# A hand-written order of steps exchanged: contiguous PSUM reads, fewer folded rows, two summed units, five output folds on GpSimd

## The chip, the cores and the metric

One NeuronCore of a Trainium2 chip runs the kernel. The metric is the device time in microseconds (us). Beside it stands the span, from the first to the last instruction of one profiled execution. The engines are TensorE (PE in the profile; PEld is its weight load), VectorE (DVE), ScalarE (ACT), GpSimd (POOL) and SyncE (SP, which here only issues DMAs).

## The reference

`x` has 2048 rows and 1024 columns in bf16. Two spectral filters are applied to it and mixed by a gate for each row:

```
g = sigmoid((x * gate_w).sum(-1, keepdims=True))
a = irfft2(rfft2(x) * (A_w_r + 1j * A_w_i))     # A_ref(x, A_w_r, A_w_i)
b = irfft2(rfft2(x) * (B_w_r + 1j * B_w_i))     # B_ref(x, B_w_r, B_w_i)
return g * a + (1 - g) * b
```

## The kernel before, in words

All transforms are products with constant matrices. Columns are folded so that even and odd frequencies (`par` 0 and 1) are handled apart, and the frequencies along the rows are split into 8 units for each parity, 16 units `n` in all (0 to 7 even, 8 to 15 odd).

The work is a list of tokens, `ORDER`, written out by hand. `run` (L587) takes them one by one and emits each step's instructions; each engine then runs its own in that order, waiting only for its data and its buffers. So the list fixes the order within each engine and each DMA queue, not the times. A token is a letter, its indices and, behind the colon, the engines of its copies out of PSUM or of its sum (A ScalarE, V VectorE, Q GpSimd). The steps are these:

- `V` (L277): a row block of `x` is folded by VectorE, a sum and a difference of its halves (L280, L281). `r` and `f` (L284, the same code under two letters): first transform of one row block, both parities; 16 matmuls of 128 columns if folded (L297), 16 of 256 if not (L306). `E`/`O`: the same for two row blocks, even and odd parity apart, 32 matmuls of 128 columns each (L309). Results are cast to `y`, two casts a token.
- `y`, `h`, `g`: gate weights (nine small VectorE operations, L322 to L333), the gate's own transform (32 matmuls and a small DMA by GpSimd, L341 to L347), the sigmoid and its table `EAB` (L350 to L361).
- `F` (L365): second forward transform of a unit into `T`, two casts; for even units GpSimd first negates a column of the weights (L369). `d` (L417): the edge columns of even units, small matmuls and two small VectorE operations (L430), which must follow GpSimd's negation. `G` (L382): third forward transform into `X`, two casts.
- `c` (L407): the complex product with both filters' weights, one VectorE operation over 4096 elements of each partition, into a buffer `p`. `a` (L434): sums two of a unit's four products on VectorE (L439), after which `i.0` and `i.1` each leave out one of four terms of matmuls (L448), 8 matmuls in all.
- `i` (L442): first inverse transform, part 0 or 1 of a unit, two casts into `rl`; after part 1 a DMA writes the unit to DRAM (`sc`, L461).
- `q` (L467): fetches a quarter of four units back from DRAM in another layout, on SP's queue. `q1.1.x` needs units 12 to 15.
- `j` (L475): second inverse transform with the gate table, of parity and row group v (0 to 7), two casts into `V`. `k` (L489): third inverse transform, into a `p` buffer; then `s` (L541), the fold: a difference and a sum of 128x512 each (L551), after which the `p` buffer is free. `D` (L508): third and fold in one on PE, for odd parity, two casts (four half ones for v 7, of which one stays in PSUM). `t` (L553): sum and difference of the even and the odd part, then the output DMA.
- `w`: loads of weights whose buffers must first come free; `l`: a late constant (`IGU`, L252).

A `k` token comes in two forms. With `H` (L493) the two operands of the fold lie in two banks; one is cast to SBUF, through a view with a break in it (L501, L502), and the other is read by the fold straight from PSUM. Without `H` both are cast to SBUF, each from one whole bank, and the fold reads SBUF only:

```
apart = eng[0] == "H"
...
po = ps[r][:, s * 256:s * 256 + 256] if apart else ps[s][:, r * 256:r * 256 + 256]
...
if apart:
    evac(eng[1], cs[:, :, 0, :], pv[0])
    CSs[par, v] = cs[:, :, 0, :], pv[1]
else:
    evac2(eng, cs.rearrange("p s r d -> p s (r d)"), ps)
```

`BANKS` names the PSUM bank (of 8) for each use in turn, and `SLOTS` the buffer for each use of `T`, `X` (2 buffers each), `p`, `V` and `rl` (4 each); both are listed for one ORDER. In `p`, the first 16 uses are the products and the last 11 the `k` tokens. Weights and constants come on SP's queue in the order of L234 to L251.

Of the kernel before, what the change touches and what calls it, by code (L numbers as in the profile page):

```python
# [11 lines left out]
S = 2048  # L12
# [14 lines left out]


ORDER = """
V0 V1 V3 f0:AA f1:VA r2:AA V4 f3:VA V7 r5:AV V9 f4:AA r6:VA f7:VA r8:VA f9:VA r11:AA V13 r10:VA r12:AV f13:AA E14:VA y  # L30
O14:VA F0:AA F1:AA d0 G0:AA F2:AA d1 c0 G1:AA F3:AA d2 c1 G2:AA h F4:AA d3 G3:AA i0.0:AA i0.1:AA w7 c2 d4 c3 F5:AV
G4:AA i1.0:AA i2.0:VA c4 i2.1:AV d5 G5:AA i1.1:VA F6:AA F7:AA d6 w9 G6:AA i3.0:AA c5 i3.1:AV d7 F8:AA w8 c6 g0 i5.0:AA
G7:AV G8:AA w15 i5.1:AV q0.0.1 w14 c7 i6.0:AA q0.0.3 F9:AA F10:AA i4.0:AA c8 i6.1:VA i7.0:AA G9:AV G10:AV i4.1:VA
i7.1:AA c10 F11:AA q0.0.0 F12:AV c9 g1 G11:AA q0.0.2 c11 F13:AA G12:AA q0.1.0 i10.0:AA i9.0:AA i8.0:VA q0.1.3 i10.1:VV
i9.1:AA c12 i8.1:AA i11.0:VA G13:AA q0.1.1 q0.1.2 F14:VA F15:AA j0.0:AA c13 G14:AA i12.0:AV G15:AA i12.1:AA i11.1:AA
c14 c15 i13.0:AA i13.1:AA i14.0:AV a15.1:V i14.1:VV k0.0:HA j0.3:AA i15.0:AV i15.1:AV j0.2:AV j0.5:AA s0.0:V l q1.0.0
k0.3:HA j0.1:AA q1.1.0 s0.3:V j0.4:VA k0.5:HA j0.7:AA q1.0.1 s0.5:V k0.1:HA q1.1.1 k0.4:HA j0.6:AA s0.1:V k0.2:HA
s0.4:V q1.0.2 q1.1.2 k0.7:AA k0.6:HA j1.0:AA q1.1.3 s0.2:V j1.1:VA s0.6:V q1.0.3 k1.0:AA s0.7:V k1.1:HA s1.0:V j1.2:AA
j1.3:AA t0.2 s1.1:V D2:AA j1.4:AA k1.3:AA t2.2 t1.2 j1.5:AA s1.3:V D4:AA t3.2 t4.2 j1.6:AA D5:AA t5.2 D6:AA j1.7:AA
t6.0:S t6.1:S D7:AAAP t7.0:A t7.1:S  # L40
"""


# [1 line left out]


BANKS = """
01234567013245760321564371052634710562437162057143057623057146257146251427306517306514273065142763051427630154
62073154620731546207315426701354270615342706135427061354027364107236410752643071265401326470152647031564703125
64703125647  # L50
"""

SLOTS = {"T": "010101010101010101001010", "X": "0101010101001010", "p": "012302132103102130213021301",
         "V": "30123012302301230123", "rl": "0123012301231023102310321032103"}


def _bf16np(a):
# [99 lines left out]
def gated_mix(ctx, tc, x_in, we_in, wo_in, first_in, out):  # L157
    nc = tc.nc
    cn = make_constants()
    dr = {n: nc.inline_tensor(a, name=f"cst_{n.lower()}").ap() for n, a in cn.items() if n not in ("F1", "SG")}  # L160
# [13 lines left out]
    slots = {t: [wk.tile([P, w], BF16, name=f"{t}_{k}") for k in range(n)] for t, (n, w) in width.items()}  # L174
    order = {t: iter(v) for t, v in SLOTS.items()}

# [19 lines left out]
    F1 = const.tile([P, 208], BF16, name="f1")  # L196
# [10 lines left out]
    WF = const.tile([P, NT, 3, 64], BF16, name="wf")  # L207
    WI = const.tile([P, NT, 4, 64], BF16, name="wi")
# [5 lines left out]
    y = [Y[:, par] for par in range(2)]  # L214
# [3 lines left out]
    def load_w(n):  # L218
        par, u = n // NU, n % NU
        if n == 7:  # L220
            w = XP[0][:, 0:2064]
        elif 10 <= n < 14:
            w = wod[n - 10][:]
        else:
            k = {8: 0, 9: 1, 14: 2, 15: 3}.get(n, n)
            w = RP[k // 2][:, 2064 * (k % 2):2064 * (k % 2) + 2064]
        w = w[:, 0:8 * PIT[par]].rearrange("p (t a m) -> p t a m", t=2, a=4)
        nc.sync.dma_start(w, w_in[par][u])
        Ws[n] = w
# [4 lines left out]
    nc.sync.dma_start(fdv(0), dr["FD"][:, 0])  # L234
    nc.sync.dma_start(WF[:, 0:4], dr["WF"][:, 0:4])
    load_w(0)
    nc.sync.dma_start(WI[:, 0:4], dr["WI"][:, 0:4])
    load_w(1)
    load_w(2)
    nc.sync.dma_start(WF[:, 4:16], dr["WF"][:, 4:16])  # L240
    load_w(3)
    nc.sync.dma_start(WI[:, 4:16], dr["WI"][:, 4:16])
    load_w(4)
# [420 lines left out]
```

## Time and profile before

| | |
|---|---|
| time, median of 3 runs | 107.3 us (106.96 to 108.08) |
| profiled execution, its own time | 107.58 us |
| its span | 105.8 us |
| TensorE clock granted, mean | 0.996 |
| PE, ACT, DVE, POOL busy | 96.9, 93.6, 90.7, 10.1 us |
| DMA | 37.06 MB, mean 350 GB/s |

Busy time is a union: a PE that is marked busy can be waiting for a PSUM bank inside a matmul. In the timeline a row `start, length, engine, line, operation, out<-in, count` merges neighbours, and the square bracket gives the idle time ahead of it and what ended it. The mean of one instruction is longer than the step from one start to the next, because neighbours overlap.

### The profile page before, as it was taken

What the parts mean: (1) busy time and instruction counts of PE and PEld (TensorE: products, weight loads), DVE (VectorE), ACT (ScalarE), POOL (GpSimd) and SP (SyncE); (2) the same over time, 40 slices, a digit from 0 to 9 for tenths busy, and PEclk for the clock granted to TensorE, in tenths of its full rate; (3) what the DMA queues carried; (4) which work ended last, traced back from release to release, by engine and by line L of the source; (5) the groups of instructions that cost most, each with busy time, mean ns of one, the idle gap of its engine ahead of it and who ended that gap; (6) DMA issues with size and microseconds to landing.
All of it is one profiled execution on the core that took longest, in us unless ns stands there. A gap on an engine that the chain in (4) does not pass through costs nothing. (4 is left out here: it accounts for less than half of the span.)

```text
span 105.8 us, 3917 instructions
## 1 busy us (share of the span) xinstructions
PE 96.9 (92%) x1606; PEld 66.5 (63%) x1608; DVE 90.7 (86%) x141; ACT 93.6 (89%) x187; POOL 10.1 (10%) x14
## 2 busy tenths in 40 slices
PE   5999999969999999999999999999999698999740
PEld 2299998635655766655765567667898485754520
DVE  1399877388999989999999999999989969899870
ACT  5069999997999999999999999999999888999730
POOL 1000001179880000000000000000000000000000
PEclk9999999999999999999999999999999999999998
DMA  2999999999999999999999799969999899967993
GB/s 50 395 421 421 386 358 353 413 428 396 398 405 409 401 375 359 395 356 345 386 373 403 223 376 379 373 249 340 321 278 298 338 353 418 397 259 321 389 352 120
DMA packets 16737, 37.06 MB, mean 350 GB/s; under 512 B 1612, under 2 KB 10448, under 8 KB 15696
## 3 DMA queue, kind: packets, MB, share of 16 engines
q1 hardware_dynamic: 16128, 36.37, 92.3%
q10 hardware_dynamic: 560, 0.45, 1.3%
q8 instruction: 12, 0.20, 0.7%
q14 instruction: 5, 0.04, 0.1%
q0 software_dynamic: 32, 0.00, 0.0%
HBM read 24.23 MB, written 12.58 MB: 348 GB/s over the span
## 5 line engine op out<-in xcount | busy, mean ns | idle before, releaser
L453 PE MATMUL pt<-p,wi 64*64 64x512 bf16 x504 | 30.1, 377 | 0.2 <-DVE rl L265 0.2
L263 ACT CAST rl<-pt 128x512 bf16<-128x512 f32 x47 | 25.9, 732 | 0.1
L415 DVE TENSOR_TENSOR p<-X,ro 128x4096 bf16<-128x4096 bf16 x11 | 25.2, 2297 | 0.4 <-ACT X L263 0.3
L263 ACT CAST T<-pt 128x512 bf16<-128x512 f32 (+1 forms) x40 | 21.8, 636 | 0.9 <-PE pt L532 0.5
L453 PEld LDWEIGHTS <-wi 64*64 64x64 bf16 x504 | 15.3, 106 | 10.4 <-issue 0.9
L263 ACT CAST V<-pt 128x512 bf16<-128x512 f32 x29 | 17.3, 748 | 1.1 <-PE pt L483 1.1
L263 ACT CAST X<-pt 128x512 bf16<-128x512 f32 x29 | 16.8, 682 | 0.1
L375 PE MATMUL pt<-fd,y 128*128 128x256 bf16 x128 | 15.9, 273 | 0.0
L263 ACT CAST y<-pt 128x512 bf16<-128x512 f32 x21 | 10.9, 649 | 3.9 <-PE pt L297 3.4
L375 PEld LDWEIGHTS <-y 128*128 128x128 bf16 x128 | 11.6, 98 | 4.2 <-issue 2.9
L265 DVE CAST rl<-pt 128x512 bf16<-128x512 f32 x17 | 11.3, 683 | 0.0
L498 PE MATMUL pt<-ig,V 128*128 128x256 bf16 x88 | 10.8, 273 | 0.0
L369 POOL TENSOR_SCALAR ro<-ro 128x8 bf16<-128x8 bf16 x7 | 8.7, 1244 | 21.4 <-DMA ro<-in_we_dram 21.4
L574 DVE TENSOR_TENSOR rl<-wo,T 128x1024 bf16<-128x1024 bf16 (+1 forms) x16 | 8.9, 620 | 0.6 <-ACT T L263 0.6
L394 PE MATMUL pt<-T,wf 64*64 64x512 bf16 (+2 forms) x192 | 9.4, 307 | 0.0
L263 ACT CAST p<-pt 128x512 bf16<-128x512 f32 x14 | 9.4, 823 | 0.0
L551 DVE TENSOR_TENSOR wo<-p,pt 128x512 bf16<-128x512 bf16 x14 | 8.8, 682 | 0.6 <-ACT p L263 0.5
L415 DVE TENSOR_TENSOR p<-X,wo 128x4096 bf16<-128x4096 bf16 x4 | 9.1, 2285 | 0.0
L498 PEld LDWEIGHTS <-V 128*128 128x128 bf16 x88 | 8.0, 98 | 1.5 <-issue 0.4
L265 DVE CAST y<-pt 128x512 bf16<-128x512 f32 x11 | 7.2, 686 | 0.4 <-PE pt L309 0.4
L306 PE MATMUL pt<-f,xr 64*128 64x256 bf16 x112 | 7.0, 269 | 0.0
L394 PEld LDWEIGHTS <-wf 64*64 64x64 bf16 x192 | 4.7, 107 | 3.0 <-issue 0.4
(58 smaller groups left out, 97.2 us busy)
## 6 DMA issues: line engine op xcount, KB each, us to landing
sc<-rl SPq DMA_DIRECT2D x16, 512.0 KB, 5.2
xr<-sc SPq DMA_DIRECT2D x8, 512.0 KB, 6.5
ro<-sc SPq DMA_DIRECT2D x8, 512.0 KB, 6.5
ro<-in_we_dram SPq DMA_DIRECT2D x7, 516.0 KB, 9.0
xr<-in_x_dram SPq DMA_DIRECT2D x7, 512.0 KB, 6.1
out_dram<-rl SPq DMA_DIRECT2D x6, 512.0 KB, 3.1
wo<-in_wo_dram SPq DMA_DIRECT2D x4, 512.0 KB, 7.5
ro<-in_wo_dram SPq DMA_DIRECT2D x4, 512.0 KB, 6.5
```

Source lines behind the costliest of these rows:

```text
L263: nc.scalar.copy(out=out, in_=in_)
L265: nc.vector.tensor_copy(out=out, in_=in_)
L306: nc.tensor.matmul(pv[h][:, :, c, :, :].rearrange("p a e k -> p e a k"), lhsT=xs(j0, h, q), rhs=fs(h, 0, *st), start=(q == 0), stop=(q == 3))
L369: nc.gpsimd.tensor_scalar(Ws[n][:, :, :, 257:258], Ws[n][:, :, :, 256:257], -1.0, None, ALU.mult)
L375: nc.tensor.matmul(ps[tt][:, e * 256:e * 256 + 256], lhsT=y[par][:, c, e, t].rearrange("p b s k -> p (b s k)"), rhs=FD[:, par, c, e, :], s ...
L394: nc.tensor.matmul(ps[tt][ho, dst:dst + ln], lhsT=WF[hp(j), 2 * u + tt, w, :], rhs=T[hp(j), tt, src:src + ln], start=(k == 0), stop=(k == 2))
L415: nc.vector.tensor_tensor(po, xo, wo, ALU.mult)
L453: nc.tensor.matmul(ps[tt][hp(j), :], lhsT=WI[hin, 2 * u + tt, w, :], rhs=p[hin, q, tt, a::2, o:o + 256], start=(k == 0), stop=(k == len(te ...
L498: nc.tensor.matmul(po, lhsT=V[:, s, 2 * r + c, :], rhs=IG[:, par, 2 * r + c, :], start=(c == 0), stop=(c == 1))
L551: (nc.vector if eng == "V" else nc.gpsimd).tensor_tensor(ev[:, :, r, :], c_, s_, op)
L574: nc.vector.tensor_tensor(o4[:, k, h] if not isinstance(od, list) else o4[:, k.start, h], x, y_, op)
```

## The change

The list is exchanged for another one, with the banks and buffers that go with it, and two constants change places in the load order. The functions stay as they are. In numbers:

- Folded rows: 0, 1, 3, 4, 7, 9, 13 before, and 2, 5, 8, 13, 14 after. The pair that goes by `E`/`O` is rows 14 and 15 before, 10 and 11 after. `y` is first in the list.
- Summed products: unit 15 before; units 1 and 5 after.
- `k`: eight of eleven tokens have `H` before, none after.
- `s`: all eleven on VectorE before; s0.1, s0.3, s0.4, s0.6 and s0.7 on GpSimd after.
- Copies out of PSUM: ScalarE 180, VectorE 37 before; ScalarE 178, VectorE 47 after (the bank that is left in PSUM for `t7` is in neither).
- Before, j0.0, j0.3 and k0.0 stand ahead of i15.1; after, every `j` and `k` stands behind it.
- `h` and the loads `w8` and `w9` move within the list, the fetches `q1` are spread among the `j` and `k` of parity 0.

```diff
--- before.py
+++ after.py
@@ -27,17 +27,17 @@
 
 
 ORDER = """
-V0 V1 V3 f0:AA f1:VA r2:AA V4 f3:VA V7 r5:AV V9 f4:AA r6:VA f7:VA r8:VA f9:VA r11:AA V13 r10:VA r12:AV f13:AA E14:VA y
-O14:VA F0:AA F1:AA d0 G0:AA F2:AA d1 c0 G1:AA F3:AA d2 c1 G2:AA h F4:AA d3 G3:AA i0.0:AA i0.1:AA w7 c2 d4 c3 F5:AV
-G4:AA i1.0:AA i2.0:VA c4 i2.1:AV d5 G5:AA i1.1:VA F6:AA F7:AA d6 w9 G6:AA i3.0:AA c5 i3.1:AV d7 F8:AA w8 c6 g0 i5.0:AA
-G7:AV G8:AA w15 i5.1:AV q0.0.1 w14 c7 i6.0:AA q0.0.3 F9:AA F10:AA i4.0:AA c8 i6.1:VA i7.0:AA G9:AV G10:AV i4.1:VA
-i7.1:AA c10 F11:AA q0.0.0 F12:AV c9 g1 G11:AA q0.0.2 c11 F13:AA G12:AA q0.1.0 i10.0:AA i9.0:AA i8.0:VA q0.1.3 i10.1:VV
-i9.1:AA c12 i8.1:AA i11.0:VA G13:AA q0.1.1 q0.1.2 F14:VA F15:AA j0.0:AA c13 G14:AA i12.0:AV G15:AA i12.1:AA i11.1:AA
-c14 c15 i13.0:AA i13.1:AA i14.0:AV a15.1:V i14.1:VV k0.0:HA j0.3:AA i15.0:AV i15.1:AV j0.2:AV j0.5:AA s0.0:V l q1.0.0
-k0.3:HA j0.1:AA q1.1.0 s0.3:V j0.4:VA k0.5:HA j0.7:AA q1.0.1 s0.5:V k0.1:HA q1.1.1 k0.4:HA j0.6:AA s0.1:V k0.2:HA
-s0.4:V q1.0.2 q1.1.2 k0.7:AA k0.6:HA j1.0:AA q1.1.3 s0.2:V j1.1:VA s0.6:V q1.0.3 k1.0:AA s0.7:V k1.1:HA s1.0:V j1.2:AA
-j1.3:AA t0.2 s1.1:V D2:AA j1.4:AA k1.3:AA t2.2 t1.2 j1.5:AA s1.3:V D4:AA t3.2 t4.2 j1.6:AA D5:AA t5.2 D6:AA j1.7:AA
-t6.0:S t6.1:S D7:AAAP t7.0:A t7.1:S
+y r1:AV r0:AA V2 r3:VV f2:AA r4:AA V5 V8 r6:VA r7:VA r9:AA f5:VA f8:VA V13 V14 E10:AA r12:AV f13:AA r15:VA f14:AV
+O10:AA F0:AV F1:AA d0 G0:VA c0 F2:AA d1 G1:AA F3:AA d2 G2:AA w7 c1 F4:AA w8 d3 a1.0:V i0.0:AA i0.1:AA d4 c2 G3:AA
+i1.0:AA G4:AA F5:AA w9 c3 c4 h i2.0:AA i1.1:AA d5 G5:VA F6:AA c5 i2.1:AA F7:AA d6 i3.0:VA a5.1:V G6:AA i3.1:AV w14 d7
+F8:AA c6 g0 i5.0:AA i5.1:AV G7:AV G8:AA w15 F9:AV c7 F10:AA i6.0:AA q0.0.1 i4.0:VA c8 i4.1:AA G9:VA i7.0:AV i6.1:AA
+i7.1:AV G10:AA F11:AA F12:AA i8.0:AA q0.0.2 q0.0.3 q0.0.0 q0.1.2 c9 c10 G11:AA q0.1.0 i9.0:AV i8.1:VA c11 i9.1:AA
+i10.0:AA G12:AV F13:AV c12 F14:AA i11.0:AA G13:AA i10.1:AV c13 q0.1.1 F15:AA G14:AA i11.1:AV G15:AA i12.0:AA c14 c15
+q0.1.3 i13.0:VA i12.1:AA i13.1:AA g1 i14.0:AV i14.1:AV i15.0:VA i15.1:AV q1.0.1 q1.0.0 j0.2:AV q1.1.0 q1.1.1 j0.1:AA
+j0.0:VA j0.5:AA l k0.1:AV k0.2:VA j0.7:AA k0.0:VA q1.1.2 q1.0.2 s0.1:Q k0.5:VV s0.5:V j0.6:AA j0.4:AA j0.3:AV s0.0:V
+k0.6:AV s0.2:V k0.4:VA k0.3:AA k0.7:AA j1.0:VA q1.0.3 j1.1:VA j1.2:AV s0.3:Q k1.0:AV s1.0:V j1.3:AA k1.1:AA D2:AA
+q1.1.3 j1.4:AA t0.2 s1.1:V k1.3:AA t2.2 t1.2 s1.3:V s0.4:Q j1.5:AA D4:AA t3.2 t4.2 j1.6:AA s0.6:Q D5:AA t5.2 D6:AA
+j1.7:AA D7:AAAP t6.0:S t6.1:S s0.7:Q t7.0:A t7.1:S
 """
 
 
@@ -45,13 +45,13 @@
 
 
 BANKS = """
-01234567013245760321564371052634710562437162057143057623057146257146251427306517306514273065142763051427630154
-62073154620731546207315426701354270615342706135427061354027364107236410752643071265401326470152647031564703125
-64703125647
+01234567012346570132645701326457012364570146012357014657230146572346570214370654370521643705261437205614372051
+47623051476230514763205147360251473602514736025473602154372164075236410572361405273610452361704523671045236710
+45236710452
 """
 
-SLOTS = {"T": "010101010101010101001010", "X": "0101010101001010", "p": "012302132103102130213021301",
-         "V": "30123012302301230123", "rl": "0123012301231023102310321032103"}
+SLOTS = {"T": "010101010101010101010101", "X": "0101010101010101", "p": "012301231023102310231320222",
+         "V": "30123012031231203120", "rl": "01230123012301320132013201320"}
 
 
 def _bf16np(a):
@@ -234,10 +234,10 @@
     nc.sync.dma_start(fdv(0), dr["FD"][:, 0])
     nc.sync.dma_start(WF[:, 0:4], dr["WF"][:, 0:4])
     load_w(0)
-    nc.sync.dma_start(WI[:, 0:4], dr["WI"][:, 0:4])
+    nc.sync.dma_start(WF[:, 4:16], dr["WF"][:, 4:16])
     load_w(1)
     load_w(2)
-    nc.sync.dma_start(WF[:, 4:16], dr["WF"][:, 4:16])
+    nc.sync.dma_start(WI[:, 0:4], dr["WI"][:, 0:4])
     load_w(3)
     nc.sync.dma_start(WI[:, 4:16], dr["WI"][:, 4:16])
     load_w(4)
```

## The prediction

> **What bounds the kernel now.** I read the page's busy times first, then the table by stage, then the timeline, then GpSimd's own rows. (The chain that ended last reaches back only 3 us.)
>
> ```profile
> PE 96.9 (92%) x1606; PEld 66.5 (63%) x1608; DVE 90.7 (86%) x141; ACT 93.6 (89%) x187; POOL 10.1 (10%) x14
> ```
>
> Three engines are near full and GpSimd is nearly idle. Shares over the span hide stages, so next is the table by stage (start:end, length, busy us of PE, PEld, DVE, ACT, POOL, then clock, DMA share, GB/s):
>
> ```profile
> 20.00:25.00 5.00, 4.07 (x74) 2.05 (x72) 4.00 (x6) 4.41 (x9) 3.12 (x3) 1.00 1.03 414
> 30.00:35.00 5.00, 5.00 (x94) 2.96 (x87) 5.00 (x4) 5.00 (x11) 1.81 (x1) 1.00 1.03 403
> 60.00:65.00 5.00, 5.00 (x92) 3.56 (x88) 5.00 (x6) 5.00 (x12) 0.00 (x0) 1.00 0.95 352
> 80.00:85.00 5.00, 4.06 (x61) 3.50 (x60) 4.42 (x8) 4.34 (x10) 0.00 (x0) 1.00 0.88 312
> 95.00:100.00 5.00, 4.25 (x36) 2.27 (x34) 4.82 (x10) 4.54 (x10) 0.00 (x0) 1.00 0.87 351
> ```
>
> From 30 to 75 us ScalarE and VectorE are both full: they empty PSUM, and PE's matmuls wait for banks inside their own times. At 80 to 85 there is a hole. The timeline (start, duration) shows the hole and the step between casts:
>
> ```profile
> 57.58 5.19 ACT L263 CAST rl<-pt 128x512 bf16<-128x512 f32 x10
> 74.05 1.46 ACT L263 CAST rl<-pt 128x512 bf16<-128x512 f32 x2
> 84.56 1.09 PE L483 MATMUL pt<-eab,ro 128*128 128x64 bf16 x32 [0.94 <-DMA ro<-sc]
> 84.99 1.56 ACT L263 CAST V<-pt 128x512 bf16<-128x512 f32 x3 [0.66 <-PE pt L483]
> 86.13 1.28 DVE L551 TENSOR_TENSOR wo<-p,pt 128x512 bf16<-128x512 bf16 x2
> 87.32 0.75 DVE L551 TENSOR_TENSOR wo<-p 128x512 bf16<-128x512 bf16 x2
> 100.38 1.26 ACT L263 CAST T<-pt 128x256 bf16<-128x256 f32 x3 [0.26 <-ACT V L263]
> ```
>
> Ten ScalarE casts take 5.19 us, so one costs 0.50 to 0.51 in a run. The last cast of unit 15 (i15.1) ends at 75.5. It goes to DRAM and back (unit 15's fetch reaches PE at 84.56), while j0 and k0 fill the gap. From 75.5 to 101.64 ScalarE is idle for under 2 us: it bounds the tail as well, 4.16 us before the span's end. The folds show two prices: 1.28 for two with one operand in PSUM, 0.75 for two with both in SBUF. Last, GpSimd beside VectorE:
>
> ```profile
> 20.05 0.27 POOL L369 TENSOR_SCALAR ro<-ro 128x8 bf16<-128x8 bf16 x1 [2.45 <-DMA ro<-in_we_dram]
> 20.75 2.30 DVE L415 TENSOR_TENSOR p<-X,ro 128x4096 bf16<-128x4096 bf16 x1
> 21.31 1.87 POOL L369 TENSOR_SCALAR ro<-ro 128x8 bf16<-128x8 bf16 x1 [1.00 <-DMA ro<-in_we_dram]
> 23.82 2.30 DVE L415 TENSOR_TENSOR p<-X,ro 128x4096 bf16<-128x4096 bf16 x1
> 24.02 2.23 POOL L369 TENSOR_SCALAR ro<-ro 128x8 bf16<-128x8 bf16 x1 [0.83 <-DMA ro<-in_we_dram]
> ```
>
> The same tiny operation takes 0.27 alone, but 1.87 and 2.23 when a VectorE product with two SBUF inputs is running, and ends 0.13 after it each time (23.18 against 23.05, 26.25 against 26.12). GpSimd gets no read through beside such an instruction. No row shows the reverse.
>
> **The change, part by part.** The sum is made against the profiled execution (107.58 us, span 105.8); the median before is 107.3, 0.28 lower, and I apply the difference to the median.
>
> *Row stage.* Two fewer folded rows take four fold operations of 0.42 off VectorE (1.7 us) and cost PE 2 x (1.03 - 0.61) = 0.84 for 16 matmuls of 256 columns in place of 128. VectorE's cover is the input itself: rows arrive until about 14.5 and VectorE waits for them. After the last row came E14 and O14, 64 matmuls in 1.95 us; now r15, f14 and O10 come, 1.03 + 0.61 + 0.98, of which I count 0.5 as later. The gate weights (16.50 to 17.32) move to the start, where VectorE waits for the first row (3.3 us idle): nothing.
>
> *Constants and loads.* WF's big part (576 KB) goes ahead of weights 1 and 2, WI's small part (256 KB) behind them. WF's wait on PE (0.93 us at 22.71) goes. The 320 KB more ahead of weight 1 delay it 0.8 us at 414 GB/s; it then meets c0 on VectorE and its GpSimd negation waits to c0's end. d1 stands behind c0 in VectorE's order anyway, so zero is taken; without that cover up to 1 us. Weights 7, 8, 9 are asked for earlier on SP's queue; their buffers are free by c1, and SP is not held beyond that. The gate's h matmuls move from the scarce start (0.78 us ScalarE idle) to a full stretch; this is kept as margin.
>
> *Products summed.* a1 and a5 replace a15: one VectorE operation more (+0.68 by the row of a15), 8 matmuls fewer (32 take 1.91, so 0.48 off PE).
>
> *Casts up to i15.1.* Counted in the two lists behind the row stage, ScalarE goes from 110 casts to 105 (the five of j0.0, j0.3 and k0.0 move behind i15.1; two X casts go to VectorE and two rl casts come back): -2.5 us, +0.5 late start = -2.0. VectorE keeps 23 casts and 16 products, +0.68 and +0.5 late start; F0 and G0 each give it one of two casts where it was idle (3.3 us before the edge products), -1.2: 0. The two engines share one stream, so I take the mean: i15.1 ends 1.0 earlier, at 74.5; ends -2.0 and 0.
>
> *The filler and the tail, without GpSimd.* Behind i15.1 ScalarE has 51 casts for 49. With eleven D casts, three of them half size at 0.3: 48 x 0.51 + 3 x 0.3 = 25.4 us, to 99.9 if it never waits; before it was 101.64. PE's work there is close behind (j 0.5, k 0.9, D 1.7 each: 8 x 1.4 + 4 + 2.6 + 8.6 = 26.4 less 0.7 head start). j0 and k0 now fill 10.9 us of PE, so the fetch wait of 0.94 and 0.45 goes: write 4.8 and fetch 4.1 end at about 83.5. What is late next is PE itself. The eight "H" steps lose the half that stayed in PSUM: eight more casts, but 16 folds of 0.64 become folds of 0.375, and ten folds leave VectorE. VectorE's whole balance: 47 casts for 37 (+6.8), one sum (+0.7), four row folds less (-1.7), 12 folds x 0.42 = 5.0 in place of 16 x 0.68 + 6 x 0.42 = 13.4 (-8.4), so -2.6 us; ScalarE's is two casts of 180, -1.0. So far: -1.7 us.
>
> *GpSimd's folds.* Ten operations of 128x512 with two inputs. None is in the trace. Bounds: VectorE's 0.42 for the same shape below; above, GpSimd's memset (0.31 for 256 elements, 0.10 for one: 0.83 ns an element) three times over 512 elements plus the 0.27 of a small operation, 1.55. I take 1.1: two reads one after the other (0.85) plus 0.27. The Trainium skill (GPSIMD Engine Reference, "Elementwise — side-by-side cycle accounting") gives 2.6 cycles an element for such an addition; an estimate from that page is 1.1 to 1.2 us, and the sum would be the same.
>
> Their place: s0.3 can't start before k0.3 is cast (10.2 us after i15.1, the 20th cast); s0.4, s0.6 and s0.7 stand behind it on GpSimd and are ready, so eight operations run without a gap. And k1.0, k1.1 and k1.3 all use p buffer 2, which s0.3, s1.0 and s1.1 must have emptied: that is the wait that the change adds, and ScalarE's D2, j1.4 and the rest queue behind it. What a VectorE instruction pays when it meets a running GpSimd fold has no row: nothing if only GpSimd yields, one GpSimd operation each if the block holds both ways. I take the second, as the only rows on the pair show a whole instruction waited out. Taking turns, in us after i15.1: s0.3 10.2 to 12.4; s0.4 to 14.6; s1.0's first half 14.6 to 15.0; GpSimd to 16.1; second half to 16.5. k1.1's cast could begin at 14.3: 2.2 lost. GpSimd to 17.6, t0.2 to 18.2, GpSimd to 19.3, t0.2 to 19.9, GpSimd to 21.0, s1.1 to 21.8. k1.3's cast could begin at 19.5: 2.3 lost. Together +4.5, ends 0 and about +7 (by 1.55 an operation).
>
> Sum: -1.7 + 4.5 = +2.8 us: span 108.6, against the median 107.3 + 2.8 = 110.1.
>
> The Trainium skill (SBUF — State Buffer, "Who interferes with whom") says that a VectorE instruction with two SBUF inputs and a GpSimd instruction that reads SBUF exclude each other for the whole instruction, whichever starts first. This trace agrees for GpSimd as the loser (+0.13 after the product's end) and shows no case of the other; by that rule the result is again 110.1.
>
> **Rivals.**
> - *VectorE isn't held by GpSimd.* For it: no VectorE product is longer beside GpSimd (2.30 with, 2.29 without), though those GpSimd operations were 0.27 and came second. Then only s0.3 before k1.0 counts (12.4 against 12.75: fits) and the gain stays: 107.3 - 1.7 = 105.6, to 106.6 if PE idles 1 us. Faster. It decides if a VectorE fold beside a GpSimd one still takes 0.42.
> - *The block is short.* VectorE keeps its turn for both halves of a fold, or a GpSimd fold takes 0.8. With pairs: s1.0 to 15.35, t0.2 to 17.7, s1.1 to 19.6; lost 1.05 + 1.2 = 2.3, so +0.6: 107.9.
> - *The start slips*: the late weight 1 holds d1 and with it F's banks for the 1 us above, and i15.1 ends at 75.5 again. Behind it the tail as summed: 107.3 + 3.8 = 111.1. Against it: d1 stands behind c0 anyway.
>
> **How the numbers follow.** Taking turns 0.42 (own range 108.5 to 112.0), short block 0.23 (107.0 to 108.6), not held 0.30 (105.2 to 106.8), slip 0.05. A measurement of this kernel tells about 1% (1.07 us) from no change. Faster: 0.25 of the not-held case. Same: 0.05 of it and 0.15 of the short block. Slower: 0.42 + 0.08 + 0.05 = 0.55. The range 105.2 to 112.0 takes in the three main cases and their bounds.
>
> **What would show it.** Right: GpSimd folds of 1.0 to 1.2 us; VectorE rows at L551 and L574 stretched to over 1 us, ending just after a GpSimd fold; ScalarE idle before its p casts, released by VectorE, at 88 to 97; i15.1's cast ending near 74.5; no fetch wait before j1.0; no WF wait near 22. Wrong: two-operand folds at 0.42 beside GpSimd ones, GpSimd folds under 0.7, or i15.1 ending after 75.5.

## The result and the profile after

The changed kernel takes 110.2 us (median of 6 runs), the one before 107.57 in the same comparison: a ratio of 1.026 (95% interval 1.022 to 1.029). It is slower by about what was forecast. Some executions of this kernel are slower ones at a lower granted clock: times here and below are medians of all executions, ratios leave those out. The profiled execution has a span of 108.1 us.

GpSimd's rows for the folds in the timeline after (start, length):

```profile
77.03 2.26 POOL L551 TENSOR_TENSOR wo<-p 128x512 bf16<-128x512 bf16 x2 [38.07 <-ACT p L263]
83.75 10.19 POOL L551 TENSOR_TENSOR wo<-p 128x512 bf16<-128x512 bf16 x8 [4.46 <-ACT p L263]
```

s0.1's two operations take 2.26 us while VectorE only empties PSUM, so 1.13 each (1.1 was taken). An estimate from the 2.6 cycles an element of the Trainium skill (GPSIMD Engine Reference, "Elementwise — side-by-side cycle accounting") was 1.1 to 1.2, and the trace agrees. The other eight run without a gap from 83.75 (84.7 was forecast) and take 10.19, where eight times 1.13 would be 9.0. VectorE in the same stretch, and on to the end:

```profile
85.98 0.69 DVE L265 CAST V<-pt 128x512 bf16<-128x512 f32 x1 [0.56 <-PE pt L483]
87.02 0.69 DVE L265 CAST p<-pt 128x512 bf16<-128x512 f32 x1 [0.35 <-PE pt L498]
87.82 2.00 DVE L551 TENSOR_TENSOR T<-p 128x512 bf16<-128x512 bf16 x2
89.85 3.08 DVE L574 TENSOR_TENSOR rl<-wo,T 128x1024 bf16<-128x1024 bf16 x2
93.03 1.53 DVE L551 TENSOR_TENSOR T<-p 128x512 bf16<-128x512 bf16 x2
94.48 2.48 DVE L574 TENSOR_TENSOR rl<-wo,T 128x1024 bf16<-128x1024 bf16 x4
96.89 0.75 DVE L551 TENSOR_TENSOR T<-p 128x512 bf16<-128x512 bf16 x2
97.67 5.15 DVE L574 TENSOR_TENSOR rl<-wo,T 128x1024 bf16<-128x1024 bf16 x10
```

Three things are to be seen. A cast out of PSUM keeps its 0.69 beside GpSimd. s1.0, t0.2 and s1.1, which have two SBUF operands, take 2.00, 3.08 and 1.53 for two operations; alone they take 0.75, 1.25 and 0.75 (the last fold here, and half of 2.48), so 3.9 us are lost. And from 87.82 to the end of t5.2 no row has idle time ahead of it. ScalarE in the same stretch stands idle before its casts of k1.1 and k1.3, as forecast:

```profile
89.92 1.07 ACT L263 CAST p<-pt 128x512 bf16<-128x512 f32 x2 [1.76 <-PE pt L532]
94.67 1.07 ACT L263 CAST p<-pt 128x512 bf16<-128x512 f32 x2 [1.71 <-PE pt L483]
```

The profile names PE as what ended these waits, but the casts begin 0.10 and 0.11 after s1.0 and s1.1 have ended (89.82 and 94.56), the folds that empty p buffer 2. A narrower window of the timeline shows each engine's turns:

```profile
88.20 1.33 POOL L551 TENSOR_TENSOR wo<-p 128x512 bf16<-128x512 bf16 x1
```

```profile
88.44 1.37 DVE L551 TENSOR_TENSOR T<-p 128x512 bf16<-128x512 bf16 x1
89.85 1.52 DVE L574 TENSOR_TENSOR rl<-wo,T 128x1024 bf16<-128x1024 bf16 x1
```

The GpSimd operation from 88.20 to 89.53 also waits for the first of s1.0's two operations on VectorE (87.82 to 88.52); the second one, from 88.44, ends at 89.81, 0.28 behind the GpSimd operation. They take turns, one instruction each. The chain that ended last, 3 us long before, now runs back along VectorE through these very instructions, and ahead of them to the fetch that waits for unit 15:

```profile
79.51 5.68 DMA ro<-sc
...
85.32 0.63 PE pt L483 x16
...
87.82 0.12 DVE T L551
...
88.44 1.38 DVE T L551
...
89.85 3.09 DVE rl L574 x2
...
94.56 1.26 DVE rl L574 x3
```

### The profile page after: what moved, and what is told of

Read it like the earlier page. It is cut to its first block, busy times and chain, and to the rows that moved or that the text cites. A ratio compares the mean times of both kernels' runs of the same rounds, so it can differ in the third digit from the quotient of the medians.

```text
span 108.1 us, 3915 instructions
## 1 busy us (share of the span) xinstructions
PE 97.9 (91%) x1598; PEld 67.3 (62%) x1600; DVE 92.7 (86%) x138; ACT 93.2 (86%) x185; POOL 21.2 (20%) x24
## 4 chain that ended last, share of the span: by engine, by line
PE 56%; DVE 15%; DMA 14%; issue 6%; ACT 5%; SPq 0%; DVEq 0%; ACTq 0%
PE pt L453 19%; PE pt L375 13%; DMA sc<-rl 9%; PE pt L306 8%; DVE rl L574 7%; PE pt L394 6%; DMA ro<-sc 5%; PE pt L195 3%; DVE T L551 3%; ACT y L263 2%; DVE rl L265 2%; PE pt L341 2%; DVE rl L565 2%; ACT V L263 1%; PE pt L297 1%
## 5 line engine op out<-in xcount | busy, mean ns | idle before, releaser
L263 ACT CAST rl<-pt 128x512 bf16<-128x512 f32 x49 | 29.8, 878 | 0.0
L551 POOL TENSOR_TENSOR wo<-p 128x512 bf16<-128x512 bf16 x10 | 12.5, 1276 | 42.5 <-ACT p L263 42.5
L263 ACT CAST V<-pt 128x512 bf16<-128x512 f32 x26 | 14.1, 636 | 0.4 <-PE pt L483 0.4
L369 POOL TENSOR_SCALAR ro<-ro 128x8 bf16<-128x8 bf16 x7 | 7.0, 993 | 22.8 <-DMA ro<-in_we_dram 22.8
L263 ACT CAST p<-pt 128x512 bf16<-128x512 f32 x14 | 7.8, 637 | 3.6 <-PE pt L532 1.8
L574 DVE TENSOR_TENSOR rl<-wo,T 128x1024 bf16<-128x1024 bf16 (+1 forms) x16 | 10.7, 729 | 0.1
L265 DVE CAST rl<-pt 128x512 bf16<-128x512 f32 x15 | 9.8, 683 | 0.1
L306 PE MATMUL pt<-f,xr 64*128 64x256 bf16 x144 | 8.6, 270 | 0.3 <-ACT y L263 0.3
L394 PEld LDWEIGHTS <-wf 64*64 64x64 bf16 x192 | 5.9, 106 | 4.0 <-issue 0.9
L306 PEld LDWEIGHTS <-xr 64*128 64x128 bf16 x144 | 6.7, 94 | 2.2 <-DMA xr<-in_x_dram 1.3
```

The lines of the kernel that those rows point to most:

```text
L263: nc.scalar.copy(out=out, in_=in_)
L265: nc.vector.tensor_copy(out=out, in_=in_)
L306: nc.tensor.matmul(pv[h][:, :, c, :, :].rearrange("p a e k -> p e a k"), lhsT=xs(j0, h, q), rhs=fs(h, 0, *st), start=(q == 0), stop=(q == 3))
L369: nc.gpsimd.tensor_scalar(Ws[n][:, :, :, 257:258], Ws[n][:, :, :, 256:257], -1.0, None, ALU.mult)
L394: nc.tensor.matmul(ps[tt][ho, dst:dst + ln], lhsT=WF[hp(j), 2 * u + tt, w, :], rhs=T[hp(j), tt, src:src + ln], start=(k == 0), stop=(k == 2))
L551: (nc.vector if eng == "V" else nc.gpsimd).tensor_tensor(ev[:, :, r, :], c_, s_, op)
```

## Experiments

The comparison kernel "before" was timed anew beside each group, on the same chip: medians 107.72, 107.56 and 107.25 us in the three groups, and 107.40, 107.50 and 107.12 over the executions that the ratios use. The first group is x1, x3, x4 and x5, the second x2, y1, y4 and y6, the third y8, y9 and the doubled x4.

**All folds on VectorE** (x1). Five tokens:

```diff
-s0.1:Q   s0.3:Q   s0.4:Q   s0.6:Q   s0.7:Q
+s0.1:V   s0.3:V   s0.4:V   s0.6:V   s0.7:V
```

> The changed list with its five GpSimd folds given back to VectorE at the same places; nothing else differs. After: 110.2 us; the three VectorE sums that met GpSimd folds took 2.00, 3.08 and 1.53 us for two operations each, against 0.75, 1.25 and 0.75 alone, 3.9 us in all, and VectorE has no idle time from 87.8 to 102.8 us. If the loss came through ScalarE's wait for p buffer 2 alone, the time is 105.6 to 106.6 us. If VectorE's own queue is the bound of the tail, it saves the 3.9 but takes four late folds of 0.7 (2.8) in the same stretch, and the time is 108.0 to 109.5. If the list itself is worse than the one before, GpSimd apart, it is about 110.

Measured: 108.65 us, ratio 1.012 (1.005 to 1.019). That is 1.55 us below the change, in the case "VectorE's own queue". By these medians GpSimd accounts for somewhat more than half of the loss; 1.2% against before (1.25 us of 107.40) stays with the rest of the list.

In the profiled execution that rest arises ahead of s1.0. Unit 15's last cast ends at 74.90, 0.6 earlier than before, yet s1.0 begins 1.13 later than before (87.99). From there to VectorE's last end it takes 14.97 us, against 14.83 before.

```profile
87.44 0.75 DVE L551 TENSOR_TENSOR wo<-p 128x512 bf16<-128x512 bf16 x2
88.31 0.58 ACT L263 CAST p<-pt 128x512 bf16<-128x512 f32 x1 [1.06 <-DVE wo L551]
89.12 0.76 DVE L551 TENSOR_TENSOR T<-p 128x512 bf16<-128x512 bf16 x2
```

ScalarE's cast of k1.0 waits 1.06 us until s0.3 (87.44) has emptied p buffer 2. Ahead of it PE waits 0.70 and 0.38 us for units to come back from DRAM.

**Buffers of their own for k1.0, k1.1 and k1.3** (x3):

```diff
-        cs = take("p", 2, 2064)[:, 0, 0:1024].rearrange(...)
+        a, b = {(1, 0): (0, 1024), (1, 1): (1, 0), (1, 3): (1, 1024)}.get((par, v), (0, 0))
+        cs = take("p", 2, 2064)[:, a, b:b + 1024].rearrange(...)
```

> The changed kernel with its GpSimd folds, but k1.0, k1.1 and k1.3 are written to parts of the p buffer that nobody else uses, so that their casts no longer wait for s0.3, s1.0 and s1.1. The VectorE sums beside GpSimd folds must stay stretched (about 2.0, 3.1, 1.5 us for two). If ScalarE's waits for p buffer 2 (1.76 and 1.71 us before its p casts) carry the loss to the end, as the prediction put it, the time falls by about 3.5 to 106.7 us. If VectorE's queue carries it, the time stays at 109.5 to 110.3 us and ScalarE waits at another buffer (T) instead.

Measured: 111.75 us, 1.040 (1.035 to 1.045): not faster, even 1.5 slower. ScalarE no longer waits before its p casts, but it is stopped a little later at T, by VectorE's t steps:

```profile
92.13 1.11 ACT L263 CAST p<-pt 128x512 bf16<-128x512 f32 x2
93.08 1.14 ACT L263 CAST V<-pt 128x512 bf16<-128x512 f32 x2
97.73 1.07 ACT L263 CAST T<-pt 128x512 bf16<-128x512 f32 x2 [3.51 <-DVE rl L575]
```

So buffer 2 isn't what carries the loss; VectorE's queue is, and whatever ScalarE needs from it next. The three VectorE sums take 2.75, 3.09 and 0.76, 6.60 us in all, as after the change (6.61).

That this run is slower than the change, and not equal, comes from a later stage, where PE does the eight matmuls of D6 (the first two below) more slowly. The other line of each pair is the granted clock in tenths over 40 equal slices of the span. The change:

```profile
98.67 0.60 PE L532 MATMUL pt<-ig,V 128*128 128x512 bf16 x2 [0.48 <-ACT V L263]
PEclk9999999999999999999999999999999999999998
```

This run:

```profile
99.35 1.03 PE L533 MATMUL pt<-ig,V 128*128 128x512 bf16 x2 [2.96 <-ACT V L263]
PEclk9999999999999999999999999999999999995898
```

From 100 to 102 us the granted clock is 0.50, after PE stood idle for 2.96 us; after the change it is 1.00 there. From D6's start to the next step's it takes 3.34 us (to 102.69) in place of 1.74 (98.67 to 100.41): 1.6 more, about what the medians differ by. The four executions of this run have a mean clock of 0.981 to 0.984, the six of the change 0.996 to 1.000. Without the lower clock it would be about as slow as the change, an estimate from these rows.

**GpSimd additions that nobody waits for** (x4, x4 doubled), on top of x1, started when s0.2 is done:

```diff
+        if (par, v) == (0, 2):
+            jk = const.tile([P, 2, 256], BF16, name="jk")
+            for _ in range(8):                 # 16 in the second kernel
+                nc.gpsimd.tensor_tensor(jk[:], ev[:, :, 0, :], ev[:, :, 1, :], ALU.add)
```

> All folds on VectorE, and eight additional GpSimd additions of 128x512 with two SBUF inputs whose result nobody reads, started when s0.2 is done (about 83 us); they are extra work. No instruction waits for them, so only the shared way to SBUF can cost. If GpSimd's reads hold VectorE's two-input instructions, each of some 6 to 8 met operations pays up to 1.1 us, but from s0.2 on VectorE also has folds to be met: 3 to 7 us over the run without them. If they don't hold VectorE, the time is that of the run without them within 0.5 us.

Measured: 112.05 us, 1.043 (1.038 to 1.048), 3.4 over x1, though no later step waits for them. Then sixteen:

> All folds on VectorE as in the run at 108.65 us, and sixteen free GpSimd additions in place of eight (which gave 112.05, +3.4); extra work that nobody reads. If each addition holds up VectorE's next two-input operation, the meetings go on past 94 us through the t steps, where VectorE has two-input work without a break: another eight meetings at 1.1 us, 119 to 121 us. If the cost were a single hold at the start, 112 to 113 us.

Measured: 119.55 us, 1.113 (1.105 to 1.120): 10.9 over x1. The second eight cost 7.5 where the first eight cost 3.4, since they meet t steps without a break: from the start of s1.1 to that of s0.4 VectorE takes 3.76 us with eight additions (94.76 to 98.52) and 11.22 with sixteen (94.79 to 106.01). Four VectorE operations of t2.2 and t1.2 in that run, which take 2.48 us after the change:

```profile
97.20 6.30 DVE L578 TENSOR_TENSOR rl<-wo,T 128x1024 bf16<-128x1024 bf16 x4
103.43 2.66 DVE L551 TENSOR_TENSOR T<-p 128x512 bf16<-128x512 bf16 x2
```

6.30 less 2.48 is 0.96 lost at each of the four meetings.

**GpSimd writes alone** (x5), in place of the additions:

```diff
+            jk = const.tile([P, 1024], BF16, name="jk")
+            nc.gpsimd.tensor_scalar(jk[:, 0:8], ev[:, 0, 0, 0:8], -1.0, None, ALU.mult)
+            for _ in range(10):
+                nc.gpsimd.memset(jk[:], 0.0)
```

> As the run with the free additions, but GpSimd does one tiny read and then ten memsets of 128x1024, which only write SBUF (by the row of 128x256 in 0.31 us about 0.9 us each, some 9 us in all); extra work that nobody waits for. If any GpSimd instruction holds VectorE, 3 to 7 us over the run with all folds on VectorE; if only its reads do, the same time within 0.5 us, and VectorE's sums keep 0.42 and 0.69 us.

Measured: 108.61 us, 1.008 (1.004 to 1.012), the same as x1. GpSimd is busy for 10 us over the same stretch, and VectorE's sums keep their lengths:

```profile
84.31 10.03 POOL L556 MEMSET jk<- 128x1024 bf16 x10
```

```profile
89.95 0.76 DVE L551 TENSOR_TENSOR T<-p 128x512 bf16<-128x512 bf16 x2
90.75 1.29 DVE L579 TENSOR_TENSOR rl<-wo,T 128x1024 bf16<-128x1024 bf16 x2
```

So it is not GpSimd's being busy, nor its writes; its reads are what is left. That is the rule of the Trainium skill (SBUF — State Buffer, "Who interferes with whom"): two SBUF inputs on VectorE against a GpSimd instruction that reads SBUF, not one that only writes it. These runs agree in both halves: additions cost 3.4 us, memsets nothing that can be told from x1.

**Where the folds stand.** Two on GpSimd as the change has them, three back on VectorE (x2):

```diff
-s0.4:Q   s0.6:Q   s0.7:Q
+s0.4:V   s0.6:V   s0.7:V
```

> The changed kernel with s0.1 and s0.3 on GpSimd as they are, and s0.4, s0.6 and s0.7 on VectorE at their places. GpSimd then runs at 77 to 79.3 and 83.75 to 86.0 us, while VectorE casts out of PSUM only. If the six GpSimd operations behind them are what costs: no stretched VectorE sum, one fold (0.75 us) less on VectorE than in the run with all folds there, 107.6 to 108.6 us. If the mere use of GpSimd costs, about 109.5.

Measured: 108.28 us, 1.007 (1.004 to 1.009). Both GpSimd folds take 2.26 and 2.27, as when alone, and VectorE's sums are not stretched. Then the two earliest folds on GpSimd and the others of even parity early on VectorE (y1):

```diff
-k0.0:VA ... s0.1:Q k0.5:VV s0.5:V ... s0.0:V k0.6:AV s0.2:V k0.4:VA k0.3:AA k0.7:AA j1.0:VA
+k0.0:VA s0.1:Q s0.2:Q ... k0.5:VV ... k0.6:AV s0.5:V s0.0:V k0.4:VA s0.6:V k0.3:AA s0.4:V k0.7:AA s0.3:V j1.0:VA
...
+j1.1:VA s0.7:V
```

> The changed list, but GpSimd gets only the two earliest folds, s0.1 and s0.2 (done by about 81.6 us), and the six other folds of even parity go to VectorE behind them, each near its k and ahead of the first t. If a GpSimd fold costs only where VectorE has two-input work at the same time, nothing is stretched here: VectorE loses two folds (1.5 us) against the run with all folds on VectorE (108.65), and its late folds move out of the bound stretch: 107.0 to 107.9 us. If GpSimd folds cost wherever they stand, 109 or more.

Measured: 107.73 us, 1.003 (1.000 to 1.006), 0.9 below x1 and within a measurement's reach of before. So how many folds GpSimd takes, and where they and the late folds stand, decides between 2.6% and next to nothing; y1 changes all of this at once and does not show which counts.

**Parts alone, on the kernel before.** Plain k steps for the eight with H (y4):

```diff
-k0.0:HA (and seven more)
+k0.0:AV
```

> The kernel before with its eight H steps made plain ones, one cast on ScalarE and one on VectorE (the unbroken reads alone). VectorE: 8 casts more (4.8 us) and 16 folds at 0.375 in place of 0.64 (4.2 less), so +0.6; ScalarE: 8 casts of one whole bank in place of 8 broken ones, at most 0.3 us less each. Where VectorE bounds, +0.6; where ScalarE does, up to -2: 106.5 to 108.4 us. If this part were the reason for the rest of the loss (108.65 with all folds on VectorE), it would show 108.5 or more.

Measured: 107.76 us, 1.000 (0.996 to 1.004): no difference. The two constants exchanged as in the change (y6):

> The kernel before with only the two constants' places exchanged as in the change. The 0.93 us wait for WF at 22.7 us goes, weight 1 comes 0.8 us later. I costed the edit at nothing, since VectorE's queue stands between both and the rest: 107.7 within 0.5 us. If the late weight holds the start, +0.5 to +1.0; if the WF wait counted, -0.5 to -0.9.

Measured: 107.49 us, 0.997 (0.993 to 1.001): no difference; PE has no wait for WF left near 22 us, and it was worth nothing.

**Both parts, and with two early folds on GpSimd** (y9, y8), to see whether a version beats both kernels:

> The same without GpSimd folds: plain k steps and the load order alone. Both parts by themselves gave 1.0001 and 0.9973 of before, so 107.1 to 107.7 us. It is the comparison for the run with two early folds on GpSimd.

> The kernel before with plain k steps (the same time as before, 1.0001), the load order of the change, and its two earliest folds, s0.0 and s0.3, on GpSimd, at about 73 to 75.5 and 77 to 79.5 us; VectorE's folds s0.5 then begins near 78 and may meet half a GpSimd fold. VectorE does 1.5 us less between 75 and 84. If VectorE's queue sets when j1 is reached, up to 1 us faster: 106.5 to 107.2 us. If the fetch of the last units sets it (ScalarE waits 0.70 and 0.77 us there now), the gain stops there: 107.2 to 107.6 us.

Measured: y9 107.92 us, 1.005 (1.001 to 1.009), where no loss was expected; y8 107.59, 1.001 (0.998 to 1.005). The two early GpSimd folds cost nothing (y8 and y9 overlap) and give nothing that can be told from before, as the fetch case said: PE still waits 1.4 us in all for the units' return in y8. No version here beats the kernel before.

## Why the prediction held, step by step

- **GpSimd's fold**: 1.1 taken, 1.13 measured alone.
- **VectorE held by GpSimd, taking turns**: right. The rows before showed only GpSimd waiting; the reverse was the step without a row, and x4, its double and x5 show it by itself. The rivals "not held" and "VectorE keeps its turn for both halves" are out: the second half of s1.0 paid 1.37 for 0.42.
- **How it reaches the end**: the step that failed. The prediction let ScalarE's wait for p buffer 2 carry 4.5 us. The waits are there (1.76 and 1.71 us before p casts), but x3 removed them and gained nothing. VectorE's queue itself is full from 87.8 on. From the start of s1.0 to VectorE's last end it takes 14.83 us before (87.99 to 102.82) and 17.22 after (87.82 to 105.04), 2.39 longer: 3.9 are lost in the three sums, but VectorE's waits in that stretch fall from 1.18 to 0.23 us, and s1.1 is 0.53 shorter without an operand in PSUM.
- **"-1.7 without GpSimd"**: no run has this term by itself, since none takes the folds off VectorE without reads by GpSimd. The way that was forecast for it, ScalarE ending earlier, is not borne out: of the 0.8 us that i15.1 gained only 0.17 is left at the start of s1.0, and with all folds on VectorE (x1) the list is 1.2% slower than before. The prediction's tail balance had counted ScalarE and PE, and VectorE only as a total. So that 2.8 came out right was partly luck: the stall was 0.6 smaller than summed, and what offsets it came mostly from VectorE's shorter waits and the cheaper s1.1.
- **i15.1**: 74.5 forecast; its last VectorE casts end at 74.69 (72.21 + 2.48), against 75.51 before. Right; the rival "the start slips", which had 75.5, is out.
- **Row stage**: 0.5 late was taken; the first T cast begins at 18.30 in place of 17.37, so 0.9. Mis-sized.
- **Loads**: costed at nothing, y6 agrees. **Fetch wait**: gone before j1.0, but 0.60 us is left at 85.32, before j1.2, against 0.94 and 0.45. That fetch took 5.68 us, to 85.19, where 4.1 and an end at about 83.5 were forecast.
- **Broken reads**: before y4, up to 0.3 us more was allowed for a broken cast; y4 gained nothing. Their mean falls from 823 to 637 ns in the change, but a mean includes overlap.

What stays open is the last 1.2% of x1. Its profile puts the loss ahead of s1.0, with k1.0's cast waiting for s0.3. y1, which has s0.3 ahead of j1.0, is 0.9 us faster, which fits, but it also moves other folds and gives one more early fold to GpSimd; moving s0.3 alone was not tried, nor the row stage's 0.9.

## What to carry to other kernels

Before a sum is handed to an idle GpSimd, ask what VectorE does in that very stretch: beside casts out of PSUM it is free, beside sums with two SBUF operands each VectorE instruction can pay a whole GpSimd instruction, about 1 us here. The place in a list doesn't delay GpSimd: late tokens whose data are ready run early, in one block, into whatever VectorE is then doing. And when a stall is found at one engine, check with a separate buffer whether it carries the loss or only shows it.

## What was not expected of the hardware

The free additions' cost grows faster than their number (3.4 us for eight, 10.9 for sixteen), because it is set by the two-operand VectorE work that they meet. And a ScalarE cast through a view broken into two runs of 256 cost no more than a whole one: two broken ones take 0.96 us from their start to the next cast's (79.93 to 80.89 before the change), two whole ones 0.97 (89.92 to 90.89 after it). The granted clock, too, can depend on how long PE waits: it fell to 0.50 behind a wait of 2.96 us in x3 and of 4.31 us in the run with sixteen additions, and stayed at 1.00 behind one of 1.40 us after the change. That the wait is the cause was not tested by itself.
